# Attention and MLP on one core: from half-array matmuls to the full 128x128 array, with a list-scheduled order

## The chip, the cores and the metric

The kernel runs on one core of a Trainium2 chip. The metric is device time in microseconds (us). Each time below is a median of several executions of the same build. Engines: PE is TensorE (matrix multiply), PEld its weight loads, DVE is VectorE, ACT is ScalarE, POOL is GpSimd, SP is SyncE, which only issues DMA transfers here.

## The reference, cut to what matters

Eight batch elements, eight heads, 576 tokens, head dimension 64. Attention with a relative position bias is followed by an MLP with a "snake" activation over all 4,608 tokens.

```python
scores = q @ k.T / 8 + bias_table[bucket(|i - j|)]      # per batch element and head
attn = softmax(scores); y = attn @ v
x = y as (4608 tokens, 512)
h = x @ w_in                                            # 512 -> 2048
g = h + sin(alpha * h)**2 / (alpha + 1e-9)
out = g @ w_out                                         # 2048 -> 512
```

The bias depends on the distance only and is constant beyond 128. So the kernels subtract that constant and multiply exp(scores) by exp(bias) in a band around the diagonal. The multipliers stand in a tile `m2[p, head, x]`, whose row p is the head's table shifted by p.

## The kernel before

Scores are kept transposed (keys on partitions). Two heads form a pair, p; z is the head in the pair. A head has only 64 dimensions, so each score matmul uses half of the rows of the array, and the value matmuls half of its columns. Two partners are issued together, one for each half.

```python
# scores: 64 rows x 128 columns of the array, z = 0 and 1 in the two halves
nc.tensor.matmul(out=sc[:, z, 0:HS],
    lhsT=kT[64*z : 64*z+64, p, 128*c : 128*c+128],
    rhs=qT[64*z : 64*z+64, p, HS*w : HS*w+HS], start=True, stop=True)
# ... one exponential for both heads: 128 x 576
# values, then sums (by a block of ones): 128 rows x 64 columns
nc.tensor.matmul(out=av[64*z : 64*z+64, part, 0:HS],
    lhsT=vt[:, c, 2*p+z, :] if part == 0 else ones,
    rhs=u[:, base+c, z, :], start=(c == 0), stop=False)
# ... reciprocal of the sums as exp(-ln(sum)) on ScalarE, product on VectorE
# MLP, one batch element (576 tokens) at a time, per 128 of the 2048 features:
nc.scalar.activation(out=s16, in_=hps[:, :, 0:HS], func=AF.Sin, scale=alphaT[:, f:f+1])
nc.vector.tensor_tensor(out=sq, in0=s16, in1=s16, op=ALU.mult)
nc.vector.scalar_tensor_tensor(out=o, in0=sq, scalar=inv_a[:, f:f+1], in1=hps[:, :, 0:HS], ...)
# bias tile: table to DRAM, read back as overlapping rows, reversed by a matmul
nc.sync.dma_start(out=e1x.ap(), in_=e_sb)
nc.sync.dma_start(out=jr, in_=bass.AP(tensor=e1x.ap().tensor, ..., ap=[[1,128],[EW,H],[1,XW]]))
```

The output projection (`mo`, 128x128 weights, 512 columns) of earlier tokens fills fixed slots between the attention matmuls. Keys and queries of the first element are transposed on TensorE, those of the others by DMA.

The softmax here doesn't subtract the row's maximum and nothing guards it: scores larger than these inputs give would overflow.

Of the kernel before, what the change touches and what calls it, by code (L numbers as in the profile page):

```python
# [16 lines left out]
AV_SLOTS = (1, 2, 6, 7)  # L17
FILL_SLOTS = (0, 3, 5, 8)
RES = 1
EXP_SET = "natural_log_exp_and_others"  # L20

# [12 lines left out]
def kernel(  # L34
# [21 lines left out]
    HS = S // 2  # L56
    SI = 6
# [11 lines left out]
    e1x = nc.dram_tensor("e1x", [H, EW], F16, kind="Internal")  # L69
# [3 lines left out]
    for x in range(EW - 1):  # L73
        phi_np[bt[abs(x - 255)], x] = 1.0
    phi_h = nc.inline_tensor(phi_np, "phi_const")
    jmat = nc.inline_tensor(np.eye(128, dtype=np.float16)[::-1].copy(), "jrev")
    idm = nc.inline_tensor(np.eye(SPB, dtype=np.float16), "ident")

    kTs = [sgl.tile([128, NP, S], F16, name=f"kT{i}") for i in range(2)]
    qTs = [sgl.tile([128, NP, S], F16, name=f"qT{i}") for i in range(2)]  # L80
    vs = [sgl.tile([128, 5, H, D], F16, name=f"v{i}") for i in range(2)]
    ones = sgl.tile([128, D], F16, name="ones")
# [3 lines left out]
    w_out16 = sgl.tile([128, NF, DM], F16, name="w_out16")  # L86
# [8 lines left out]
    j_sb = sgl.tile([128, 128], F16, name="j_sb")  # L95
    id_sb = sgl.tile([SPB, SPB], F16, name="id_sb")

    natx = tp.tile([SPB, NF * 2 * S], F16, name="natx", tag="g2", bufs=2)
    NW = 2 * H * SI * D
    nat = natx[:, 0 : 2 * NW].bitcast(F32).rearrange(  # L100
        "s (kq h x) -> s kq h x", kq=2, h=H
    )
    natb = natx[:, 2 * NW : 3 * NW].rearrange(
        "s (kq p i two d) -> s kq p i two d", kq=2, p=NP, i=SI, two=2
    )

    def new_g2():
        return tp.tile([128, NF, 2 * S], F16, name="g2", tag="g2", bufs=2)

    def new_xT():  # L110
        return tp.tile([128, NP, S], F16, name="xT", tag="xT", bufs=2)

    def new_u():
        return tp.tile([128, 9, 2, HS], F16, name="u", tag="u", bufs=2)

    def new_ln():
        return tp.tile([128, HS], F32, name="lnd", tag="lnd", bufs=2)

    def new_rd():
        return tp.tile([128, HS], F32, name="rd", tag="rd", bufs=2)  # L120

    def new_s16():
        return tp.tile([128, 2, HS], F16, name="s16", tag="s16", bufs=3)

    def new_sq():
        return tp.tile([128, 2, HS], F16, name="sq", tag="sq", bufs=2)

    def new_outs():
        return tp.tile([128, DM], F32, name="outs", tag="outs", bufs=3)

    def new_sc():
        return ps.tile([128, 2, 512], F32, name="sc", tag="sc", bufs=2)

    def new_av():
        return ps.tile([128, 2, 512], F32, name="av", tag="av", bufs=1)

    def new_mo():
        return ps.tile([128, DM], F32, name="mo", tag="mo", bufs=2)

    def load_nat(p):  # L140
        for kq, src in ((0, k), (1, q)):
            nc.sync.dma_start(
                out=nat[:, kq, 2 * p : 2 * p + 2, :],
                in_=src[0, 2 * p : 2 * p + 2].rearrange("h (p i) d -> p h (i d)", i=SI),
            )
# [8 lines left out]
    def load_kqT(t):  # L154
        nc.sync.dma_start_transpose(out=kTs[t % 2][:, :, :], in_=staged_k.ap()[t])
        nc.sync.dma_start_transpose(out=qTs[t % 2][:, :, :], in_=staged_q.ap()[t])

    def load_v16(t):
        dst = vs[t % 2]
        for c in range(4):  # L160
            nc.gpsimd.dma_start(  # L161
                out=dst[:, c, :, :],
                in_=v[t, :, 128 * c : 128 * c + 128, :].rearrange("h s d -> s h d"),
            )
        vh = v[t, :, 512:576, :].rearrange("(hp two) s d -> two s hp d", two=2)
        dh = dst[:, 4, :, :].rearrange("p (hp two) d -> p two hp d", two=2)
        for par in range(2):
            nc.gpsimd.dma_start(
                out=dh[64 * par : 64 * par + 64, par, :, :], in_=vh[par]
            )  # L170
# [5 lines left out]

    def load_w_out16():
        src = moe_w_out.rearrange("(f p) n -> p f n", p=128)
        for fh in range(4):
            nc.gpsimd.dma_start(  # L180
                out=w_out16[:, 4 * fh : 4 * fh + 4, :], in_=src[:, 4 * fh : 4 * fh + 4, :]
            )

    def cast_pair(p, eng):
        for kq in range(2):
            i_ = nat[:, kq, 2 * p : 2 * p + 2, :].rearrange("s two (i d) -> s i two d", i=SI)
            o = natb[:, kq, p]
            if eng == "pool":
                nc.gpsimd.tensor_copy(out=o, in_=i_)
            elif kq == 0:  # L190
                nc.vector.tensor_copy(out=o, in_=i_)
            else:
                nc.scalar.activation(out=o, in_=i_, func=AF.Copy)
# [7 lines left out]
    )  # L201
    nc.sync.dma_start(out=id_sb, in_=idm.ap())
    load_nat(0)
    nc.sync.dma_start(out=phi_sb, in_=phi_h.ap())
    nc.sync.dma_start(out=j_sb, in_=jmat.ap())
    for p in range(1, NP):
        load_nat(p)
    load_v16(0)
    for p in range(1, NP):
        cast_pair(p, "pool")  # L210

    nc.vector.memset(ones, 1.0)
    cast_pair(0, None)
# [4 lines left out]
    nc.vector.tensor_copy(out=e_sb, in_=eps_[0:H, 0:EW])  # L218
    nc.sync.dma_start(out=e1x.ap(), in_=e_sb)
    jr = tp.tile([128, H, XW], F16, name="jr", tag="u", bufs=2)  # L220
    nc.sync.dma_start(
        out=jr,
        in_=bass.AP(tensor=e1x.ap().tensor, offset=e1x.ap().offset,
                    ap=[[1, 128], [EW, H], [1, XW]]),
    )
    with nc.allow_non_contiguous_dma(reason="alpha transpose load"):
        nc.sync.dma_start(
            out=alphaT,
            in_=bass.AP(tensor=moe_alpha.tensor, offset=moe_alpha.offset,
                        ap=[[1, 128], [128, NF]]),  # L230
        )

    load_w_in16()
    stage_kq(1)
    load_v16(1)
    load_w_out16()
    load_kqT(1)

    def tr_pair(p):
        for kq, dst in ((0, kTs[0]), (1, qTs[0])):  # L240
            pt = new_sc().bitcast(F16)
            for i in range(SI):
                nc.tensor.transpose(
                    out=pt[:, i // 3, SPB * (i % 3) : SPB * (i % 3) + SPB],
                    in_=natb[:, kq, p, i],
                    identity=id_sb,
                )
            o = dst[:, p, :].rearrange("d (p two i) -> d two i p", two=2, i=3)
            pin = pt[:, :, 0:HS].rearrange("d two (i p) -> d two i p", i=3)
            if kq == 0:  # L250
                nc.vector.tensor_copy(out=o, in_=pin)
            else:
                nc.scalar.activation(out=o, in_=pin, func=AF.Copy)

    def build_m2():
        for h2 in range(NP):
            pm = new_sc()
            for z in range(2):
                nc.tensor.matmul(
                    out=pm[:, z, 0:XW], lhsT=j_sb, rhs=jr[:, 2 * h2 + z, :],  # L260
                    start=True, stop=True,
                )
            nc.vector.tensor_copy(out=m2[:, 2 * h2 : 2 * h2 + 2, :], in_=pm[:, :, 0:XW])
        me = m2.rearrange("p (hp two) x -> p two hp x", two=2)
        nc.vector.tensor_copy(out=mh[0:64, :, :], in_=me[0:64, 0, :, 0:192])
        nc.vector.tensor_copy(out=mh[64:128, :, :], in_=me[64:128, 1, :, 64:256])

    UN = [(0, 0), (0, 1), (0, 2), (0, 3), (None, 4), (1, 0), (1, 1), (1, 2), (1, 3)]
    PEND = None

    pairs = {}
    xTs = {}
    g2s = {}

    def qk_unit(t, p, n):
        if n == 0:
            pairs[(t, p)] = new_u()
        u = pairs[(t, p)]
        kT, qT = kTs[t % 2], qTs[t % 2]
        w, c = UN[n]  # L280
        sc = new_sc()
        if c < 4:
            for z in range(2):
                nc.tensor.matmul(  # L284
                    out=sc[:, z, 0:HS],
                    lhsT=kT[64 * z : 64 * z + 64, p, 128 * c : 128 * c + 128],
                    rhs=qT[64 * z : 64 * z + 64, p, HS * w : HS * w + HS],
                    start=True, stop=True,
                )
        else:  # L290
            for w0 in range(2):
                for z in range(2):
                    w_ = w0 ^ z
                    nc.tensor.matmul(  # L294
                        out=sc[64 * z : 64 * z + 64, w_, 0:HS],
                        lhsT=kT[64 * z : 64 * z + 64, p, 512:576],
                        rhs=qT[64 * z : 64 * z + 64, p, HS * w_ : HS * w_ + HS],
                        start=True, stop=True,
                    )
        nc.scalar.activation(  # L300
# [201 lines left out]
```

## Time and profile before

| | us |
|---|---|
| median of the kernel before | 559.1 |
| one repetition (attention + MLP of one element) | 60 to 64 |
| attention stage / MLP stage | 39.4 / 20.9 |
| end of the first repetition | 105.5 |
| one head pair in attention | 9.27 |

The windows view gives the busy time of each engine in a stretch between two table loads of ScalarE. The first stretch here is attention, the second the MLP of the same element.

```profile
core 0: us, PE busy (x) PEld busy (x) DVE busy (x) ACT busy (x) POOL busy (x), PEclk, DMA share, GB/s
...
230.50:269.90 39.40, 37.81 (x309) 16.32 (x307) 16.13 (x42) 31.65 (x59) 2.03 (x3) 1.00 0.08 28
269.90:290.80 20.90, 17.75 (x126) 12.05 (x125) 17.73 (x31) 13.04 (x18) 7.20 (x6) 1.00 1.80 142
```

In attention PE is busy for 37.8 of 39.4 us. But busy is not the same as multiplying. The timeline of part of one pair has start, duration, engine, line, operation, tiles, and xN for N merged instructions. The time from one line's start to the next line's start is what a group costs; its own duration also holds the tail that overlaps the next group (0.30 us against 0.23 for the first line).

```profile
247.18 0.30 PE L284 MATMUL sc<-qT_69,kT_67 64*128 64x288 f16 x2
247.41 1.04 PE L396 MATMUL mo<-w_out_76,g_2065 128*128 128x512 f16 x4
248.38 0.30 PE L284 MATMUL sc<-qT_69,kT_67 64*128 64x288 f16 x2
248.61 1.04 PE L396 MATMUL mo<-w_out_76,g_2065 128*128 128x512 f16 x4
249.58 0.30 PE L284 MATMUL sc<-qT_69,kT_67 64*128 64x288 f16 x2
249.81 0.68 PE L331 MATMUL av<-u,v_71 128*64 128x288 f16 x8
250.42 0.30 PE L284 MATMUL sc<-qT_69,kT_67 64*128 64x288 f16 x2
```

In a run without other matmuls between them, 512 columns take 0.216 us each (80 in 17.28 us at the end of the kernel). Four should take 0.86 us; here 0.97 us pass until the score pair starts. The two score matmuls run at the same time (the pair lasts 0.30 us, one of them 0.293) and should take 0.12 us to the next start; they take 0.23. Something costs 0.11 us at each of these changes of shape (64\*128, 128\*64, 128\*128).

At the start, ScalarE does nothing from 16.7 to 37.3 us. A group's line in the lines view has the mean duration after its busy time; the second fence shows two groups of copies.

```profile
37.27 0.65 ACT L300 ACTIVATE u<-sc 128x576 f16<-128x576 f32 x1 [20.60 <-PE sc L284]
```

```profile
L253 ACT ACTIVATE qT_68<-sc 128x576 f16<-128x576 f16 x4 | 8.3, 2080 | 3.7 <-PE sc L243 3.7
...
L251 DVE COPY kT_66<-sc 128x576 f16<-128x576 f16 x4 | 8.2, 2062 | 0.4 <-PE sc L243 0.4
```

These copies take transposed keys and queries out of PSUM and write 2-byte elements 12 bytes apart: 2.06 us for 576 columns.

### The profile page before, as it was taken

The numbers are of one execution on the slowest core, as the hardware profiler recorded it, in microseconds if no ns is written. First come the engines' busy times: TensorE is split into PE (matmuls) and PEld (weight loads), VectorE is DVE, ScalarE is ACT, GpSimd is POOL, SyncE is SP. The second block draws the span as 40 slices with busy tenths as digits, with TensorE's granted clock in tenths as the row PEclk, the third lists the DMA queues.
The fourth block names the chain that finished last, engine by engine and source line by source line (L and its number), as shares of the span: only waits on it lengthen the run. The fifth ranks groups of instructions, "written<-read, shape, count | busy, mean of one in ns | idle before, by whom it ended". The sixth has DMA issues, their size and how long they took to land.

```text
span 559.6 us, 9036 instructions
## 1 busy us (share of the span) xinstructions
PE 475.8 (85%) x3577; PEld 242.6 (43%) x3577; DVE 284.1 (51%) x592; ACT 369.6 (66%) x602; POOL 79.7 (14%) x80
## 2 busy tenths in 40 slices
PE   1227778799879999899879998899889998899897
PEld 0013335444553446444544446344544455344553
DVE  2054437743583337743683439543683439433760
ACT  3126666688667876788667865787668865787631
POOL 4823005000600023000600051000300000000000
PEclk9999679999998999999999999999999999899999
DMA  9999919300990049710990179210900110001001
GB/s 177 193 163 172 166 29 165 20 30 28 81 152 19 20 58 146 66 39 20 124 107 20 39 63 152 37 39 20 147 1 20 39 39 1 15 25 38 1 20 75
DMA packets 148171, 38.70 MB, mean 69 GB/s; under 512 B 138361, under 2 KB 143009, under 8 KB 148129
## 3 DMA queue, kind: packets, MB, share of 16 engines
q0 software_dynamic: 105056, 17.17, 41.2%
q1 hardware_dynamic: 43072, 20.95, 19.1%
q8 instruction: 28, 0.46, 0.3%
q14 instruction: 15, 0.11, 0.1%
HBM read 37.58 MB, written 17.70 MB: 99 GB/s over the span
## 4 chain that ended last, share of the span: by engine, by line
PE 58%; DVE 23%; ACT 10%; DMA 5%; issue 2%; DVEq 0%; SPq 0%; ACTq 0%
PE mo L396 22%; PE av L331 15%; PE sc L284 9%; DVE sq L379 7%; PE av L341 4%; DVE g_627 L381 4%; DVE g_4953 L381 3%; DVE g_3510 L381 3%; DVE g_2065 L381 3%; DMA alphaT<-in_moe_alpha_dram 3%; ACT u L300 3%; PE sc L369 2%; PE sc L294 2%; ACT L432 2%; ACT lnd L351 1%
## 5 line engine op out<-in xcount | busy, mean ns | idle before, releaser
L300 ACT ACTIVATE u<-sc 128x576 f16<-128x576 f32 x288 | 180.1, 646 | 59.0 <-PE sc L284 48.8
L313 DVE TENSOR_TENSOR u<-u,m_73 128x576 f16<-128x576 f16 (+5 forms) x224 | 80.1, 358 | 100.6 <-ACT u L300 94.3
L369 PEld LDWEIGHTS <-w_in_75 128*128 128x128 f16 x1024 | 99.2, 97 | 65.7 <-issue 41.8
L369 PE MATMUL sc<-xT,w_in_75 128*128 128x288 f16 x688 | 97.8, 285 | 15.0 <-DVE xT L353 2.0
L353 DVE TENSOR_TENSOR xT<-av,rd 128x288 f16<-128x288 f32 x64 | 29.3, 458 | 72.5 <-ACT rd L352 66.0
L284 PE MATMUL sc<-qT_68,kT_66 64*128 64x288 f16 x256 | 40.4, 319 | 19.2 <-ACT u L300 9.5
L369 PE MATMUL av<-xT,w_in_75 128*128 128x288 f16 x336 | 47.9, 285 | 6.4 <-DVE xT L353 1.5
L351 ACT ACTIVATE lnd<-av 128x288 f32<-128x288 f32 x64 | 26.2, 410 | 36.5 <-PE av L341 36.5
L331 PE MATMUL av<-u,ones 128*64 128x288 f16 x512 | 46.5, 306 | 0.0
L284 PE MATMUL sc<-qT_69,kT_67 64*128 64x288 f16 x256 | 37.7, 293 | 7.9 <-ACT u L300 5.9
L284 PEld LDWEIGHTS <-kT_66 64*128 64x128 f16 x256 | 14.3, 95 | 56.6 <-issue 53.7
L396 PE MATMUL mo<-w_out_76,g_627 128*128 128x512 f16 x144 | 38.0, 388 | 0.0
L161 POOL DMA_DIRECT2D v_71<-in_v_dram x16 | 15.3, 1104 | 158.0 <-PE av L331 157.8
L396 PE MATMUL mo<-w_out_76,g_2065 128*128 128x512 f16 x144 | 37.2, 382 | 0.0
L396 PE MATMUL mo<-w_out_76,g_3510 128*128 128x512 f16 x144 | 37.1, 382 | 0.0
L396 PE MATMUL mo<-w_out_76,g_4953 128*128 128x512 f16 x144 | 34.9, 387 | 0.0
L161 POOL DMA_DIRECT2D v_70<-in_v_dram x16 | 14.3, 908 | 138.1 <-PE av L331 137.3
L284 PEld LDWEIGHTS <-kT_67 64*128 64x128 f16 x256 | 13.3, 93 | 44.8 <-issue 44.3
L402 ACT ACTIVATE outs<-mo 128x512 f32<-128x512 f32 x36 | 21.2, 590 | 14.6 <-PE mo L396 14.2
L331 PEld LDWEIGHTS <-ones 128*64 128x64 f16 x512 | 25.2, 113 | 11.1 <-issue 2.8
L352 ACT ACTIVATE rd<-lnd 128x288 f32<-128x288 f32 x64 | 28.4, 443 | 2.0
L341 PE MATMUL av<-u,ones 64*64 64x288 f16 x128 | 28.8, 309 | 0.0
(315 smaller groups left out, 564.5 us busy)
## 6 DMA issues: line engine op xcount, KB each, us to landing
out_dram<-outs SPq DMA_DIRECT2D x36, 256.0 KB, 2.0
staged_k<-in_k_dram POOLq DMA_DIRECT2D x7, 576.0 KB, 14.2
staged_q<-in_q_dram POOLq DMA_DIRECT2D x7, 576.0 KB, 17.4
v_70<-in_v_dram POOLq DMA_DIRECT2D x16, 128.0 KB, 4.6
w_in_75<-in_moe_w_in_dram POOLq DMA_DIRECT2D x4, 512.0 KB, 9.6
v_71<-in_v_dram POOLq DMA_DIRECT2D x16, 128.0 KB, 8.8
w_out_76<-in_moe_w_out_dram POOLq DMA_DIRECT2D x4, 512.0 KB, 15.9
natx<-in_k_dram SPq DMA_DIRECT2D x4, 288.0 KB, 7.8
```

The costliest lines, as they stand in the source:

```text
L161: nc.gpsimd.dma_start(out=dst[:, c, :, :], in_=v[t, :, 128 * c : 128 * c + 128, :].rearrange("h s d -> s h d"),)
L284: nc.tensor.matmul(out=sc[:, z, 0:HS], lhsT=kT[64 * z : 64 * z + 64, p, 128 * c : 128 * c + 128], rhs=qT[64 * z : 64 * z + 64, p, HS * w : ...
L300: nc.scalar.activation(out=u[:, n, :, :], in_=sc[:, :, 0:HS], func=AF.Exp, scale=0.125)
L313: nc.vector.tensor_tensor(out=io, in0=io, in1=m2[:, 2 * p : 2 * p + 2, x0 : x0 + hi - lo], op=ALU.mult,)
L331: nc.tensor.matmul(out=av[64 * z : 64 * z + 64, part, 0:HS], lhsT=vt[:, c, 2 * p + z, :] if part == 0 else ones, rhs=u[:, base + c, z, :], ...
L341: nc.tensor.matmul(out=av[64 * z : 64 * z + 64, pt, 0:HS], lhsT=(vt[64 * z : 64 * z + 64, 4, 2 * p + z, :] if pt == 0 else ones[64 * z : 6 ...
L351: nc.scalar.activation(out=ln, in_=av[:, 1, 0:HS], func=AF.Ln)
L353: nc.vector.tensor_tensor(out=xTs[t][:, p, HS * w : HS * w + HS], in0=av[:, 0, 0:HS], in1=rd, op=ALU.mult,)
L369: nc.tensor.matmul(out=hps[:, w, 0:HS], lhsT=w_in16[:, j, 128 * f : 128 * f + 128], rhs=xT[:, j, HS * w : HS * w + HS], start=(j == 0), st ...
L379: nc.vector.tensor_tensor(out=sq, in0=s16, in1=s16, op=ALU.mult)
L381: nc.vector.scalar_tensor_tensor(out=o, in0=sq, scalar=inv_a[:, f : f + 1], in1=hps[:, :, 0:HS], op0=ALU.mult, op1=ALU.add,)
L396: nc.tensor.matmul(out=mo, lhsT=g2[:, f, c0 : c0 + 128], rhs=w_out16[:, f, :], start=(f == 0), stop=(f == NF - 1),)
```

## The change

The intent is to let every matmul in the steady state use the full array. Keys are padded with zeros to 128 rows. Each head's values get 64 columns of ones beside them, so values and sums come from one matmul. All PSUM tiles are 512 columns wide (the "one-bank" buffers of the prediction). The MLP works on blocks of 512 tokens, and squares are shared by ScalarE and VectorE. The order of all instructions comes from a list scheduler in the kernel's source, with durations written into it (0.6 to 0.7 us for a copy of the kind above) and with times at which loads are counted on. The start changes too: two elements are transposed on TensorE rather than one, tokens lie 8 apart rather than 6, and the bias tile is loaded straight from SBUF.

```diff
-    kTs = [sgl.tile([128, NP, S], F16, name=f"kT{i}") for i in range(2)]
+    kzs = [sgl.tile([128, NP, 2 * S], F16, name=f"kz{i}") for i in range(2)]
-    vs = [sgl.tile([128, 5, H, D], F16, name=f"v{i}") for i in range(2)]
+    vs = [sgl.tile([128, 5, H, 2, D], F16, name=f"v{i}") for i in range(2)]
...
-    HS = S // 2
+    WIN = ((0, 384), (384, 192))
...
+                        out=sc.v[:, n * y : n * y + n], lhsT=kzs[t % 2][:, p, k0 : k0 + 128],
+                        rhs=qTs[t % 2][:, p, q0 : q0 + n], start=True, stop=True,
...
+                        out=avs[z].v[:, 0:n], lhsT=vs[t % 2][:, c, 2 * p + z, :, :],
+                        rhs=u.v[:, 8 if c == 4 else 4 * z + c, q0 : q0 + n],
...
-    nc.sync.dma_start(out=e1x.ap(), in_=e_sb)
-    jr = tp.tile([128, H, XW], F16, name="jr", tag="u", bufs=2)
...
+    for h in range(H):
+        nc.sync.dma_start(
+            out=m2[:, h, :],
+            in_=bass.AP(tensor=e_sb.tensor, offset=e_sb[h : h + 1, 127:128].offset,
+                        ap=[[e_sb.ap[0][0], 1], [-1, 128], [1, XW]]),
+        )
...
+            def lg(e, z=z):
+                nc.scalar.activation(
+                    out=ln.v[64 * z : 64 * z + 64, 0:n],
+                    in_=avs[z].v[64 - 64 * z : 128 - 64 * z, 0:n], func=AF.Ln,
+                )
```

The windows of queries change from two of 288 (`HS`), with both heads in one exponential, to one of 384 and one of 192. `lg` is the logarithm of the sums, now one per head on 64 partitions. The eight matmuls and four copies that made the bias tile from `jr` are gone.

## The prediction

> **What bounds the kernel now.** The windows view shows attention and MLP stages alternating, one pair per batch element: attention 39.4 us (230.5 to 269.9, TensorE busy 37.8, ScalarE 31.7, VectorE 16.1), MLP 20.9 us (VectorE busy 17.7, TensorE 17.8, ScalarE 13.0). Attention is bound by TensorE, the MLP by VectorE: the timeline shows its square and its combine alternating every 1.285 us, TensorE waiting.
>
> The closing output projection runs 80 matmuls of 512 columns in 17.28 us, 0.216 each. One head pair takes 9.27 us (243.55 to 252.82 in the timeline). Counting row- and column-tiled partners as concurrent, its columns (2,880 scores, 5,760 values and sums, 8,192 output projection) are worth 7.1 us at that rate. The rest is at the changes of array shape: 4 output matmuls before a score pair take 0.97, not 0.86; two concurrent 288-column scores take 0.23, not 0.12; eight half-width value matmuls 0.61, not 0.49. About 0.11 us per change, some 20 changes, 2.2 us per pair, 70 us in 32 pairs. [...]
>
> **The change.** All matmuls use the full array, so these 70 us go. Padded keys cost 2,304 columns more per pair, 31 us in all; values with ones cost the same columns. Per pair: scores and values 10,944 columns = 4.6 us, plus 10 filling output matmuls (2.2) = 6.8 us of TensorE.
>
> ScalarE becomes the limit of attention. Back-to-back exponentials of 576 start 0.54 us apart (4 in 2.28 us)[...]. Per pair: 13 of 384 at 0.375, one of 192, four half-height logarithms, two reciprocals: 6.9 us of issue. I expect 7.5, 30 us per attention stage.
>
> MLP: 512-token units, half the squares on ScalarE. TensorE 16 x 0.86 = 13.8 us plus fills; VectorE about 14 us. With fills, drain and table loads (1.28 each) I expect 21 us including transitions. One repetition: 51.5 us (before: 60 to 64; floor of TensorE's sum 46).
>
> Start: before, ScalarE waits 20.6 us at 16 to 37 us, mostly behind the alpha load (15.6 us landing) that blocks VectorE; that goes, and less small-packet staging. Against it, key and query transposes for two elements need 24 strided copies, which took 2.06 us each before; the scheduler assumes 0.6 to 0.7. I expect the first repetition to end at 83 us (before: 105.5).
>
> End: the last stage does two blocks, 1,024 tokens: 61 us of dense TensorE, against 43 before.
>
> Sum: 83 + 6 x 51.5 + 33 + 61 + 3 = **489 us**, range 470 to 515. Chances: faster by over 2% 0.97, within 2% 0.02, slower 0.01.
>
> **What would show it.** Timeline: no 0.11 us extra at changes between scores, values and projection; a pair at 7.2 to 7.9 us, ScalarE nearly gapless. Windows: attention near 30 us, ScalarE busy over 90%. MLP no longer paced by VectorE at 1.285 us. Start: strided copies near 2 us; first MLP end near 83 us. End: over 120 output matmuls at 0.216 in a row, at full clock.
>
> **What would make it wrong.** Exponentials that wait on a static order built with wrong durations (pair over 8 us, repetition over 55); copies stalling the first element beyond 90 us; weight loads not hidden behind 192-column matmuls; the four one-bank score buffers too few for the MLP's chain (over 1 us per unit)[...].

The sum: 83 + 309 + 33 + 61 + 3 = 489. The 0.375 us for an exponential of 384 columns is an estimate. Another estimate, from the trace of the kernel before: an exponential of 576 columns lasts 0.65 us and a logarithm of 288 lasts 0.41, so 192 columns fewer are worth 0.16, and 0.54 - 0.16 = 0.38. Measured in the changed kernel: 0.371.

## The result

The changed kernel took 540.2 us (539.4 to 541.2, 4 runs) against 559.1 before. The ratio of the mean times of the fast runs of the same rounds is 0.964 (95% interval 0.960 to 0.969). Ratios here are always computed so, the mean of one kernel's fast runs over that of the other's, and are not quite the ratio of the medians quoted. It is faster, but outside the predicted range of 470 to 515.

Where the time is, by the table loads of ScalarE that separate the stages in the timeline:

| Term of the predicted sum | predicted | measured | kernel before |
|---|---|---|---|
| end of the first repetition | 83 | 124.1 | 105.5 |
| six repetitions | 6 x 51.5 = 309 | 311.7 (6 x 52.0) | 371.5 |
| attention of the last element | 33 | 35.4 | 41.2 |
| last MLP stage to the end | 61 + 3 = 64 | 68.2 | 41.4 |
| sum | 489 | 539.4 | 559.6 |

Of the 50 us missing, 41 are in the first repetition. The steady state is as fast as predicted, though not stage by stage:

```profile
core 0: us, PE busy (x) PEld busy (x) DVE busy (x) ACT busy (x) POOL busy (x), PEclk, DMA share, GB/s
0.00:105.25 105.25, 45.92 (x397) 26.57 (x398) 55.29 (x70) 66.20 (x101) 42.12 (x54) 0.85 1.13 117
...
175.54:210.35 34.81, 31.94 (x199) 17.91 (x198) 18.74 (x47) 32.46 (x81) 1.01 (x2) 1.00 0.56 59
210.35:227.42 17.07, 17.07 (x80) 7.65 (x79) 14.07 (x24) 16.77 (x28) 10.66 (x11) 1.00 1.59 136
```

Attention is 34.8 us (30 predicted) with ACT busy 93%; the MLP stage is 17.1 (21 predicted, with transitions) and PE has no gap in it. The same kind of excerpt of a pair as before:

```profile
191.12 0.59 PE L648 MATMUL mo<-w_out_365,g 128*128 128x512 f16 x2
191.72 0.32 PE L472 MATMUL sc<-qT_69,kz_66 128*128 128x384 f16 x1
191.88 0.81 PE L648 MATMUL mo<-w_out_365,g 128*128 128x512 f16 x3
192.53 0.33 PE L472 MATMUL sc<-qT_69,kz_66 128*128 128x384 f16 x1
```

A score matmul of 384 columns now costs 0.16 us and three output matmuls 0.65: exactly their columns. The 0.11 us at each change is gone. At the end, 123 output matmuls run in a row, as predicted:

```profile
508.64 26.71 PE L648 MATMUL mo<-w_out_365,g 128*128 128x512 f16 x123
```

The start is another matter. These are lines of the timeline of SP, DVE and ACT; the bracket is the idle time before and what ended it.

```profile
10.73 17.95 SPq L355 DMA_DIRECT2D m_73<-e_sb  x8
...
42.22 0.35 DVE L372 COPY mh<-m_73 64x768 f16<-64x768 f16 x1 [12.00 <-DMA m_73<-e_sb]
44.09 0.36 DVE L373 COPY mh<-m_73 64x768 f16<-64x768 f16 x1 [1.52 <-DMA m_73<-e_sb]
...
48.05 2.71 ACT L383 ACTIVATE kz_66<-mo 64x512 f16<-64x512 f16 x2 [16.86 <-DVE kz_66 L385]
```

The eight loads of the bias tile start at 10.7 us and are complete at 44. DVE waits for them, its copies of the next keys stand behind that wait in its queue, and ACT waits for those. From 48 to 105 us ACT and DVE work on the copies in turns, 40 us in these 57. They take 2.7 us each where they are 576 columns long:

```profile
L383 ACT ACTIVATE kz_67<-mo 64x512 f16<-64x512 f16 x4 | 9.7, 2436 | 7.0 <-DVE kz_67 L385 6.9
...
L383 ACT ACTIVATE kz_66<-mo 64x576 f16<-64x576 f16 x3 | 8.2, 2717 | 2.1 <-PE mo L402 2.1
L385 DVE COPY qT_70<-mo 128x576 f16<-128x576 f16 x3 | 8.1, 2697 | 0.0
```

### The profile page after: what moved, and what is told of

Same layout as the page of the kernel before. It is cut to its first block, busy times and chain, and to the rows that moved or that the text cites. A ratio compares the mean times of both kernels' runs of the same rounds, so it can differ in the third digit from the quotient of the medians.

```text
span 539.4 us, 7396 instructions
## 1 busy us (share of the span) xinstructions
PE 452.9 (84%) x2610; PEld 234.6 (43%) x2610; DVE 314.7 (58%) x613; ACT 444.7 (82%) x911; POOL 100.6 (19%) x114
## 4 chain that ended last, share of the span: by engine, by line
PE 53%; ACT 31%; DVE 6%; DMA 4%; SPq 3%; issue 2%; DVEq 0%; ACTq 0%
PE sc L600 24%; ACT u L479 20%; PE mo L648 14%; PE av L539 10%; PE sc L472 5%; ACT lnd L553 4%; SPq L355 3%; DMA m_73<-e_sb 3%; ACT rd L566 2%; ACT kz_67 L383 2%; DVE xT L574 2%; DVE kz_67 L385 2%; DMA phi_sb<-phi_const 1%; DVE u L512 1%; ACT L669 1%
## 5 line engine op out<-in xcount | busy, mean ns | idle before, releaser
L479 ACT ACTIVATE u<-sc 128x384 f16<-128x384 f32 x448 | 180.6, 503 | 3.1 <-PE sc L472 1.5
L648 PE MATMUL mo<-w_out_365,g 128*128 128x512 f16 x576 | 155.2, 379 | 0.0
L600 PE MATMUL sc<-xT,w_in_75 128*128 128x512 f16 x576 | 136.1, 386 | 6.3 <-DVE xT L574 6.3
L621 DVE SCALAR_TENSOR_TENSOR g<-sq,inv_a,sc 128x512 f16<-128x512 f16 x144 | 103.2, 745 | 17.0 <-ACT sq L614 7.5
L512 DVE TENSOR_TENSOR u<-u,m_73 128x512 f16<-128x512 f16 (+1 forms) x192 | 70.2, 392 | 66.7 <-ACT u L479 64.6
L574 DVE TENSOR_TENSOR xT<-av,rd 64x192 f16<-64x192 f32 (+1 forms) x128 | 58.2, 455 | 65.4 <-ACT rd L566 63.0
L600 PEld LDWEIGHTS <-w_in_75 128*128 128x128 f16 x576 | 57.0, 99 | 78.2 <-issue 16.8
L648 PEld LDWEIGHTS <-g 128*128 128x128 f16 x576 | 55.5, 97 | 64.4 <-issue 14.1
L472 PE MATMUL sc<-qT_69,kz_66 128*128 128x384 f16 (+1 forms) x288 | 65.5, 307 | 15.8 <-ACT u L479 15.3
L539 PE MATMUL av<-u,v_71 128*128 128x384 f16 (+1 forms) x320 | 56.2, 312 | 24.9 <-DVE u L512 21.1
L472 PE MATMUL sc<-qT_70,kz_67 128*128 128x384 f16 (+1 forms) x288 | 62.4, 284 | 12.1 <-ACT u L479 11.5
L539 PEld LDWEIGHTS <-v_71 128*128 128x128 f16 x320 | 31.2, 104 | 44.7 <-issue 30.1
L539 PE MATMUL av<-u,v_72 128*128 128x384 f16 (+1 forms) x320 | 49.3, 285 | 0.4 <-DVE u L512 0.2
L472 PEld LDWEIGHTS <-kz_66 128*128 128x128 f16 x288 | 28.9, 103 | 33.1 <-issue 20.6
L472 PEld LDWEIGHTS <-kz_67 128*128 128x128 f16 x288 | 27.4, 97 | 30.6 <-issue 16.4
L539 PEld LDWEIGHTS <-v_72 128*128 128x128 f16 x320 | 29.1, 97 | 18.3 <-issue 3.9
L383 ACT ACTIVATE kz_66<-mo 64x576 f16<-64x576 f16 (+2 forms) x5 | 10.9, 2269 | 19.0 <-DVE kz_66 L385 16.9
## 6 DMA issues: line engine op xcount, KB each, us to landing
w_in_75<-in_moe_w_in_dram POOLq DMA_DIRECT2D x4, 512.0 KB, 17.1
```

The lines of the kernel that those rows point to most:

```text
L383: nc.scalar.activation(out=o, in_=i, func=AF.Copy)
L472: nc.tensor.matmul(out=sc.v[:, n * y : n * y + n], lhsT=kzs[t % 2][:, p, k0 : k0 + 128], rhs=qTs[t % 2][:, p, q0 : q0 + n], start=True, st ...
L479: nc.scalar.activation(out=u.v[:, k0 : k0 + nc_, q0 : q0 + n], in_=sc.v[:, 0 : n * nc_], func=AF.Exp, scale=0.125,)
L512: nc.vector.tensor_tensor(out=io, in0=io, in1=m2[:, 2 * p : 2 * p + 2, x0 : x0 + hi - lo], op=ALU.mult,)
L539: nc.tensor.matmul(out=avs[z].v[:, 0:n], lhsT=vs[t % 2][:, c, 2 * p + z, :, :], rhs=u.v[:, 8 if c == 4 else 4 * z + c, q0 : q0 + n], start ...
L574: nc.vector.tensor_tensor(out=xT[64 * z : 64 * z + 64, p, x0 : x0 + n], in0=avs[z].v[64 * z : 64 * z + 64, 0:n], in1=rd.v[64 * z : 64 * z ...
```

## The experiments

Twelve kernels ran. Seven explain the start and lead to a faster version (s2_hold, s2b_holdv, x1_flip, s3_copy, x2_flipcopy, x3_hold, x4_phi); five test the steady state (s4_rowtile, a1_act, a2_pe, a3_lnexp, a4_noshift). Labels are those of the runs.

### s2_hold and s2b_holdv: is the bias tile slow because other loads crowd it out?

```diff
-    load_w_in16(); ... nat2 (keys, queries of element 1) ...; load_v16(1)     # early
+    nc.gpsimd.tensor_copy(out=hold, in_=m2[:, :, 0])                          # waits for the tile
+    load_w_in16(); ... nat2 ...; load_v16(1)
```

s2b_holdv also puts `load_v16(0)` behind the wait.

> The changed kernel, but the loads of the input projection's weights and of the second element's keys, queries and values are held behind a small read of the finished bias tile, so they cannot share the DMA engines with its eight loads. In the changed kernel these eight loads land up to 44 us, and the first repetition ends at 124 us. Theory contention (the eight loads are slow because the queued weight and key loads share the engines): the bias tile lands by about 28 us, the 16.9 us idle of ScalarE at 31 us shrinks to under 5, and the time falls by 8 to 16 us, to 524 to 532. Rival 1, the loads are slow by their own nature (one source partition, 128 overlapping rows each): they still land at about 40 us, and with everything else later the time is unchanged or longer, 540 to 555. Rival 2, the first repetition is bound by the strided copies anyway: the tile lands early, but the first repetition still ends near 120 us and the time is within 4 us of 540.

> As the run before it, but the first element's values are held too. Contention: the bias tile lands still earlier, by about 22 us, at the price of values that land after it. If values are then the last to arrive, the first value matmul waits for them instead and the time is about that of the run before it, 524 to 532; if small value packets were the main contention, it is 3 to 6 us faster than that run.

Measured: 536.6 and 543.3 us. The tile was complete at 41.1 and 41.2 us instead of 44. With less traffic the eight loads were hardly sooner done, so crowding explains 3 us of the delay at most. s2_hold gained what it brought forward, 3 us in the tile and 3.6 in the time, so the tile does end last in that stretch. In s2b_holdv ScalarE then stood still for 21.4 us, as the values also came late. The chain of waits of s2b_holdv, where little else moved from about 13 to 40 us (26 to 29 GB/s in all), shows SP issuing the loads one after the other, from the fourth on in 3.1 to 3.9 us each (start, duration, what):

```profile
13.18 3.83 SPq L349
...
17.05 3.77 SPq L349
...
20.87 3.76 SPq L349
```

One load is 128 rows of 768 bytes, 98,304 bytes, in 3.8 us: 26 GB/s. All 128 rows of a load come from the single partition that holds the head's table. From 13.6 to 27.1 us the 16 DMA engines were busy for 70 to 80% of the time while they moved 29 GB/s. In x3_hold, below, eight times as many bytes, in rows of the same size, came from DRAM in 5.7 us, 138 GB/s. So the engines were held up by slow transfers, not short of them. What at the single source makes them slow, no run shows.

### x1_flip: the same tile from DRAM

```diff
+    nc.sync.dma_start(out=e1x.ap(), in_=e_sb)
+    jr = tp.tile([128, H, XW], F16, name="jr", tag="u", bufs=NBUF["u"])
+    nc.sync.dma_start(out=jr, in_=bass.AP(tensor=e1x.ap().tensor, offset=e1x.ap().offset,
+                      ap=[[1, 128], [EW, H], [1, XW]]))
...
+            nc.vector.tensor_copy(out=m2[:, h : h + 2, :], in_=jr[:, h : h + 2, ::-1])
```

The reversal works because the table is symmetric. The multiplies also wait for this copy in the scheduler's eyes.

> The changed kernel with another way to the bias tile: the 8 KB table goes to DRAM once, one load reads it back as 128 overlapping rows per head (rising addresses, as in the kernel before), and VectorE reverses the rows into the tile (four copies, some 4 us more of VectorE). In the runs so far the eight loads from one SBUF partition each took 3.8 us one after the other with nothing else moving (98,304 bytes in 3.8 us, 26 GB/s), and were not done before 41 us. [...]the read from DRAM takes 3 to 8 us, the tile is complete by 22 to 30 us, the idle 16.9 us of ScalarE shrinks to under 5, and the time falls by 10 to 16 us, to 524 to 530. Rival (the overlapping rows of 768 bytes are slow wherever they come from): tile complete after 38 us, time 537 to 545.

What was tested is whether the one source partition in SBUF is what makes the loads slow. The range of 3 to 8 us is an estimate; the same read took 4.7 us in the kernel before.

Measured: 523.0 us, 17 less than the changed kernel and slightly better than expected, although the tile came only at 33.8 us, later than the 22 to 30 expected:

```profile
33.84 1.17 DVE L374 COPY m<-jr 128x768 f16<-128x768 f16 x4 [4.96 <-DMA jr<-e1x]
```

The four reversing copies cost 1.2 us in all. The tile came 10 us sooner, and the time fell by 17: the scheduler's inputs changed too (3.9 us for the tile's work on VectorE, multiplies that wait for it), so the order of the start is another one, and ScalarE's wait of 16.9 us became one of 3.6. What the order gave is not separated. So the source, one partition of SBUF, was a cause, but with it gone something else still slowed the read; x3_hold returns to it.

### s3_copy: copies that write contiguously

```diff
-                pin = c.v[:, 0:S].rearrange("d (i p) -> d i p", i=SI)
+                pin = c.v[:, 0:S].rearrange("d (i p) -> d p i", i=SI)
-                    copy_on(e, qTs[t][:, p, :].rearrange("d (p i) -> d i p", i=SI), pin)
+                    copy_on(e, qTs[t][:, p, :].rearrange("d (p i) -> d p i", i=SI), pin)
     ... the same for the key copies
```

> The changed kernel, but the copies of the transposed keys and queries run with the token order of the output innermost: they write contiguously and read with the stride. The result stays correct. Theory stride (the 2.7 us per copy of 576 columns comes from writing single 2-byte elements 16 bytes apart): a copy takes 0.6 to 0.9 us, the 53 us from 52 to 105 us shrink by 15 to 25 us, and the time falls to 515 to 525. Rival (PSUM reading is the limit, or any strided side costs the same): copies stay at 2 to 3 us and the time within 4 us of 540.

Measured: 516.2 us, 24 less than the changed kernel, and the first repetition ended at 99.4 us instead of 124.1. The copies, in the lines view:

```profile
L385 DVE COPY qT<-mo 128x576 f16<-128x576 f16 x5 | 3.8, 752 | 0.5 <-PE mo L402 0.5
...
L383 ACT ACTIVATE kz<-mo 64x576 f16<-64x576 f16 x4 | 2.5, 635 | 0.9 <-PE mo L402 0.8
```

2.7 us became 0.64 on ACT and 0.75 on DVE. The stride is still there, on the PSUM side that is read; only the write became contiguous. So writing 2-byte elements 16 bytes apart was the cost. On ACT 576 columns took 0.64 us contiguous (s3_copy), 2.08 with 12 bytes from element to element (before) and 2.72 with 16 (the changed kernel). The 24 us also contain a second effect: in the changed kernel the granted clock was 0.71 from 52 to 105 us, where PE was busy for 31 of 53 us, and 0.82 in the first MLP stage. In s3_copy the clock was 0.990 over the whole run instead of 0.964, and that MLP stage took 16.2 us instead of 18.8, as long as in x4_phi at 1.00. So 2.6 of the 24 us were gained where no copy runs. In the attention stage before it copies and clock are not separated.

### x2_flipcopy, x3_hold, x4_phi: the repairs together

x2_flipcopy has both edits above. x3_hold also holds the weights and the second element's loads, as in s2_hold, but behind `jr`. x4_phi also requests the 32 KB table that the bias is made with before the first keys and queries.

```diff
+    nc.gpsimd.tensor_copy(out=hold, in_=jr[:, :, 0])       # x3_hold, then the loads as in s2_hold
...
+    nc.sync.dma_start(out=phi_sb, in_=phi_h.ap())           # x4_phi: moved ahead of the nat0 loads
```

> Both repairs of the start: bias tile through DRAM and copies that write contiguously. If the two causes add up (24 us for the copies as measured, 10 to 16 for the tile), 500 to 507, first repetition ending at 83 to 90 us, near the predicted 83. If the gap at 24 to 44 us that stood in the run with the contiguous copies is filled only in part because the other loads (values, weights) then arrive last, 507 to 514.

> The kernel with both repairs of the start, and in addition the weights and the second element's loads held until the read of the bias rows from DRAM has landed. In the run with both repairs that read was issued at 15.2 us and landed at 34.8, beside the weight load, and ScalarE stood still from 22 to 36 us. Theory contention ([...]the read is slowed by the queued loads): it lands by 20 to 25 us, and the time falls by 8 to 13 us, to 490 to 495. Rival (the read needs its 20 us by itself): unchanged or slower, 501 to 508.

> As the run before it, and the 32 KB one-hot table is requested ahead of the first key and query loads rather than behind them (it landed at 9.4 us and the bias chain starts with it). If the chain of the bias tile still ends last at the start, 2 to 4 us faster than that run; if the first keys and queries do, which now land later, equal within 1.5 us.

Measured: 502.7, 496.4 and 493.9 us. x2_flipcopy ended its first repetition at 86.9 us, where the prediction had put it at 83. In it the tile was still late. Two lines of DVE's timeline, the first from x2_flipcopy, the second from x3_hold:

```profile
34.89 1.17 DVE L374 COPY m<-jr 128x768 f16<-128x768 f16 x4 [16.20 <-DMA jr<-e1x]
```

```profile
20.80 1.18 DVE L376 COPY m<-jr 128x768 f16<-128x768 f16 x4 [2.08 <-DMA jr<-e1x]
```

The read was issued at 15.1 us in both. Beside the loads of the weights and of the second element it took nearly 20 us, without them 5.7. Here, with no single source partition in the way, crowding by the queued loads is the cause, which it was not in s2_hold. The time fell by 6.4 us where 8 to 13 were expected; that weights and the second element's keys now come later is a likely reason, not a tested one. x4_phi gained another 2.4 us, as expected.

x4_phi is the fastest version: a ratio of 0.880 to the kernel before (0.874 to 0.886). Its first repetition ends at 76.0 us, and its steady state is that of the changed kernel.

### s4_rowtile: do changes of array shape cost time?

```diff
-                        lhsT=kzs[t % 2][:, p, k0 : k0 + 128],
-                        rhs=qTs[t % 2][:, p, q0 : q0 + n], ...
+                        lhsT=kzs[t % 2][r0 : r0 + rn, p, k0 : k0 + 128],     # r0, rn = 64*z, 64
+                        rhs=qTs[t % 2][r0 : r0 + rn, p, q0 : q0 + n], ...    # the last 64 keys stay full
```

> The changed kernel, but the scores of the 128-key chunks go back to 64-row tiles (same outputs, same order, 8 of 9 score groups per window); values and output projection keep the full array. [...]with 8 to 12 groups of scores per pair between other matmuls, 16 to 24 changes cost 1.8 to 2.6 us per pair, less what concurrent partners save (up to 1 us); attention goes from 35 to 37 to 41 us and the time to 555 to 590. Rival (changes cost nothing and only array columns count): TensorE has less to do, the time is 535 to 541.

What it put to the test is the cost itself: about 0.11 us of TensorE at each change, as in the trace of the kernel before.

Measured: 561.1 us, 21 more, and attention 38.3 us instead of 34.8 (third repetition of each). With the same columns in the same order, and each matmul as long as in the changed kernel (0.32 to 0.33 and 0.82 us, there 0.32 to 0.33 and 0.81):

```profile
192.95 0.60 PE L650 MATMUL mo<-w_out,g 128*128 128x512 f16 x2
193.51 0.32 PE L473 MATMUL sc<-qT,kz 64*128 64x384 f16 x1
193.76 0.82 PE L650 MATMUL mo<-w_out,g 128*128 128x512 f16 x3
194.52 0.33 PE L473 MATMUL sc<-qT,kz 64*128 64x384 f16 x1
```

The lone score matmul costs 0.25 us instead of 0.16, and the three output matmuls before the next one 0.76 instead of 0.65. That is 0.09 to 0.11 us for each change, with the result unchanged. The weight loads (PEld) suggest what is lost. First s4_rowtile, then the changed kernel, each before a score matmul (194.52 and 192.53):

```profile
194.51 0.09 PEld L473 LDWEIGHTS <-kz 64*128 64x128 f16 x1 [0.42 <-issue]
```

```profile
192.31 0.10 PEld L472 LDWEIGHTS <-kz_66 128*128 128x128 f16 x1
```

With one shape the weights load 0.22 us ahead here, during the matmul before (192.31 for 192.53). At the change of shape they load only when the score matmul is due (194.51 for 194.52), and their 0.09 to 0.10 us are about what a change costs. The kernel before shows the same (both at 248.38). This reading fits these places in the traces; no run tested it on its own.

The 21 us may not all be due to the shape. In the first two of its seven later attention stages the granted clock was 0.95 and 0.96; in the changed kernel it was 1.00. Over the whole run it was 0.942 against 0.964. Six of the seven stages are 3.2 to 4.9 us longer than in the changed kernel, the last 2.3 (37.7 against 35.4). By an estimate from that shortest one, taken as undisturbed, the shapes alone cost some 16 us in seven stages, most of the 19 us that the change had gained. That the clock makes the rest was not shown stage by stage.

### a1_act and a2_pe: which engine bounds attention now?

```diff
+                for _ in range(2 if w == 0 and c in (0, 2) and z == 0 else 1):      # a1_act
                     nc.scalar.activation(out=u.v[...], in_=sc.v[...], func=AF.Exp, scale=0.125)
...
-                for y in range(nc_):
+                for y in [0, 0] if w == 0 and z == 0 else range(nc_):               # a2_pe
```

> The changed kernel with two exponentials of 384 columns per head pair done twice (same result, order otherwise unchanged): 0.75 us more ScalarE per pair, 24 us in 32 pairs. Theory (ScalarE bounds attention): the time grows by 17 to 25 us, to 557 to 565. Rival (TensorE bounds it still, or the two are balanced with slack in the static order): growth under 10 us.

> The changed kernel with five score matmuls of 384 columns per head pair done twice (same result): 0.80 us more TensorE per pair, 26 us in 32 pairs. Theory (ScalarE bounds attention, TensorE has about 1.2 us of slack per pair of 7.9): growth of 2 to 12 us, to 542 to 552. Rival (TensorE bounds attention): growth of 20 to 27 us, to 560 to 567.

Measured: 573.6 us (+33) and 542.7 us (+2.5). 26 us of added TensorE work cost 2.5 us; 24 us of added ScalarE work cost 33. So ScalarE bounds attention, and TensorE has slack there. The excess of a1_act over 24 us, outside what was expected, is in its trace: in each stage eight exponentials, as many as are repeated, start 0.53 us after the one before them, not 0.37. So they add 4.2 us to a stage and not 3.0. Four of the seven later attention stages are longer by just that, the other three by 5.5 to 5.7 us. Of the stages whose clock was read, one of the four had 1.00 and one of the three 0.96. Together the seven are 33.7 us longer.

### a3_lnexp and a4_noshift: why ScalarE takes 7.9 us per pair, not 6.9

A pair takes 7.92 us (191.12 to 199.04). The prediction summed ScalarE's issue times to 6.9. Exponentials of 384 do start 0.371 us apart, close to its 0.375, though each lasts 0.49. But around the half-height logarithms this overlap is missing. ACT's timeline in the changed kernel:

```profile
193.63 0.33 ACT L553 ACTIVATE lnd<-av 64x192 f32<-64x192 f32 x1
193.97 0.49 ACT L479 ACTIVATE u<-sc 128x384 f16<-128x384 f32 x1
194.48 0.32 ACT L553 ACTIVATE lnd<-av 64x192 f32<-64x192 f32 x1
194.83 0.49 ACT L479 ACTIVATE u<-sc 128x384 f16<-128x384 f32 x1
```

From exponential to logarithm 0.51 us pass, from logarithm to exponential 0.35, each the full duration. With median spacings of 0.53 before a single logarithm, 0.346 after one of 192, and 0.565, 0.51 and 0.507 around the two of 384, that is about 1.06 us per pair more than with overlap, and 6.9 + 1.06 = 7.96. Is it the function or the shape?

```diff
-  in_=avs[z].v[64 - 64 * z : 128 - 64 * z, 0:n], func=AF.Ln,
+  in_=avs[z].v[64 - 64 * z : 128 - 64 * z, 0:n], func=AF.Exp, scale=0.0031,    # a3_lnexp
...
-  out=ln.v[64 * z : 64 * z + 64, 0:n],
+  out=ln.v[64 - 64 * z : 128 - 64 * z, 0:n],                                   # a4_noshift
```

Both give wrong results.

> The changed kernel with the logarithm of the sums replaced by an exponential with scale 0.0031, which has about the same size (wrong result on purpose, same shapes, operands and order). In the changed kernel an exponential of 384 starts 0.371 us after the one before, but 0.53 us pass before a logarithm, and after one its whole duration passes (0.507 for 384, 0.346 for 192). Theory function (overlap of neighbouring instructions is lost where the function changes): spacings fall by about 0.13 us on either side of the eight-per-pair changes, about 1 us per pair, and the time by 15 to 32 us, to 508 to 525. Rival (the half-height logarithms lose the overlap by their shape, 64 partitions shifted by 64, or by what they wait for): the spacings stay and the time stays within 5 us of 540.

> The changed kernel with the logarithms written to the same half of the partitions that they read (wrong result on purpose: each head is divided by its neighbour's sums; shapes and order unchanged). Replacing the function left the spacings at 0.53 before and 0.507 after, so it is not the function. Theory shift (the overlap is lost because output and input lie on different partitions): spacing around a logarithm falls to about 0.37 to 0.40, the time by 15 to 32 us. Rival height (64 of 128 partitions is enough to lose it): spacings and time (within 5 us of 540) stay.

Measured: a3_lnexp 538.9 us, all spacings unchanged. The function is not the reason. a4_noshift 529.0 us, 11 less, short of the 15 to 32 expected, and for half of the logarithms only:

```profile
197.06 0.33 ACT L553 ACTIVATE lnd<-av 64x192 f32<-64x192 f32 x1
197.41 0.49 ACT L479 ACTIVATE u<-sc 128x384 f16<-128x384 f32 x1
197.80 0.31 ACT L553 ACTIVATE lnd<-av 64x192 f32<-64x192 f32 x1
198.01 0.48 ACT L479 ACTIVATE u<-sc 128x384 f16<-128x384 f32 x1
```

The second logarithm, of the head whose input and output now both lie on partitions 0 to 63, costs 0.21 us; the first, both on 64 to 127, still costs 0.35. So 64 partitions alone do not lose the overlap. What fits all four cases (0.51 and 0.35 us around the logarithms of the changed kernel, 0.35 after the first and 0.21 after the second here) is that neighbouring instructions keep it when inputs and outputs all start at partition 0, as the exponentials' do (0.371). Whether it is the start or the change of start was not tried. It is not the only way to lose the overlap: the repeated exponentials of a1_act, on the same tiles and all from partition 0, lost it too (0.53). A correct layout with this gain was not built.

## Why the prediction was wrong

- **The step that failed is "I expect the first repetition to end at 83 us"; it ended at 124.1.** Two terms of it were wrong. First, the new way to the bias tile had no cost in the prediction at all. It had noted that the alpha load's wait would go, and not that eight loads, each from one partition, came in. They moved 98,304 bytes at 26 GB/s each, 30 us together, and ended last until 44 us, where the schedule counted on the tile at 15. Replacing them gained 17 us by itself, in part perhaps by the other order (x1_flip). Second, the strided copies were listed at 2.06 us with their number, 24, but they took up to 2.7. That fits the stride, which grew from 12 to 16 bytes, but no run changed the stride alone. Their sum, 69 us with the small remainders of the keys, was not set against the time that ACT and DVE had. Making them contiguous cut the sum to 18 us and gained 24 by itself (s3_copy). Both together ended the first repetition at 86.9 us, so 37 of the 41 us are accounted for.
- **"All matmuls use the full array, so these 70 us go": right.** The changes cost 0.09 to 0.11 us each (s4_rowtile), and they are gone from the trace. One repetition was predicted at 51.5 us and measured at 52.0.
- **"ScalarE becomes the limit of attention": right** (a1_act, a2_pe). The size was off: 7.9 us per pair, not 7.5, and 34.8 us per stage, not 30. The mis-sized term is "6.9 us of issue", which took the overlap of neighbouring instructions to hold for the half-height logarithms too. About 1.06 us per pair, 4.2 per stage, were lost there.
- **"MLP ... 21 us including transitions": near, once the transitions are put where it had them.** PE ran without a gap for 17.1 us. The attention stage of 34.8 us holds four pairs of 7.92, 31.7 us, and 3.1 us of table load and last waits, which the prediction had counted with the MLP. So the pairs took 1.7 us more than the 30 predicted, and the MLP with transitions 20.2 instead of 21. The two errors had opposite signs, which is in part why the repetition came out so close.
- **"61 us of dense TensorE" at the end: near.** 68.2 us from the last table load to the end, against 64 with the 3 us added.
- **Of the listed risks, "copies stalling the first element beyond 90 us" came true.** Weight loads behind 192-column matmuls (five of these take 0.41 us from 192.72, just their columns) and score buffers in the MLP (PE has no gap) did not. The clock was 1.00 from 124.1 to 511 us.

## What to carry to other kernels

Count what matmuls really cost from start to start, and look for a fixed amount at each change of array shape (0.09 to 0.11 us here); a padded full-array matmul can be cheaper than a half-array one in the middle of other shapes (0.16 us against 0.25 in s4_rowtile). A change that speeds up the steady state must still be costed line by line in its start: where a DMA reads from (26 GB/s from one partition, 138 from DRAM), how far apart a copy writes (2.7 us at 16 bytes, 0.64 contiguous, on ACT), and which wait stands ahead of it in an engine's queue (16.9 us of ScalarE). When a repair exposes the next limit (the single source partition, then crowding), repeat the test that had failed before it.
